# Forgetting attention with a feed-forward layer: q and k loads issued by GpSimd, the short chunk in rows 64 to 127, and x, inverse sums and output rows in one DMA each

## The chip, the cores and the metric

The kernel runs on one core of a Trainium2 chip. The metric is the device time of one execution in microseconds (us); of several runs the median counts. Engine names are those of the profile: PE is TensorE's matmul side and PEld its weight loads, DVE is VectorE, ACT is ScalarE, POOL is GpSimd, SP is SyncE, which issues nearly all DMAs of the kernel before.

## The reference

Eight batches with eight heads each, 576 positions, head size 64. The attention has a decay: for each head the cumulated log of a gate f is added to the scores. Its output, as 4608 tokens of 512 numbers, goes through a feed-forward layer of width 2048.

```python
scores = scale * np.matmul(q, k.transpose(0, 1, 3, 2))
log_f = np.log(np.clip(f, 0.0001, 1.0))
cum = np.cumsum(log_f, axis=-1)
decay = cum[:, :, :, None] - cum[:, :, None, :]
scores = np.where(causal, -1000000000.0, scores + decay)
attn = np.exp(scores - np.max(scores, axis=-1, keepdims=True))
attn = attn / (np.sum(attn, axis=-1, keepdims=True) + 1e-09)
x = np.matmul(attn, v)          # then to (B*S, H*D)
h = x @ w_in
out = np.maximum(0.01 * h, h) @ w_out
```

## The kernel before

**Precision.** Products are made in float32r with each operand split into a high part (a cast) and a low part (the rest): three matmuls per product. Casts are on ACT or DVE, the subtractions that give the low parts mostly on POOL (`minus`).

**Stages.** Until about 125 us weights are loaded and split, and the first 256 tokens of three batches are done in a way of their own. Then come 64 tasks, one per head: 40 full ones (576 queries in five chunks of 64, 128, 128, 128, 128 rows), until about 745 us, and 24 short ones (three chunks of 64, 128, 128 rows, the later queries of the three batches), until about 1095 us. The rest is feed-forward alone. Between the steps of the tasks, `fill` lays pieces of the feed-forward (h, g, gh, gl, o) on the engines, by a credit that is fixed when the program is built.

**A task.** Its scores (`sc`) come chunk by chunk from TensorE, DVE adds the mask and finds the maximum (`z`, `max`), ACT takes the exponential, DVE transposes 32x32 blocks into `zt`. SP sends `zt` to DRAM (`send`: four DMAs `zd<-zt`) and fetches it back transposed over partitions (`receive`: one DMA `fixed_pl<-zd`). ACT casts it to `fixed_ph`, DVE makes the low part in `fixed_pl` (`divide`), TensorE multiplies with the values (`av`), ACT copies one part out (`y`), DVE adds (`x`). A full task does this in two pieces (0 and 1), a short one in one. After each odd task the inverse sums of its pair of heads go through DRAM (`rt`, `inv`, `rb`), `x` is multiplied by them (`normalise`) and written to `xd`, from where the feed-forward reads it.

**The next tasks' data.** In the second half of each task q and k for the task after the next are loaded into `qraw` and `kraw` (one buffer each; `load`, four DMAs of 64 rows), after ACT has cast the next task's `s` and `m` from the same buffers (`split`) and ACT and POOL have made its `fixed_s2`/`fixed_m2` (`prepare`: ACT casts, POOL subtracts).

**Order.** Each engine runs its instructions in the order in which the code is written. `todo` places each step of a task in a slot (eight slots to a task): send of piece 0 in slot 3, receive 0 and send 1 in 5, `split_next`, `load_next` and `split_v` in 6, receive 1 in 9, values in 12 and 16, `prepare_next` in 2; in short tasks send in 5 and receive in 9. A DMA that must wait stops all that SP has behind it. A DMA also takes one of eight completion semaphores in turn (DMAHW0 to 7 for SP), and waits for the DMA that had it last where nothing else has made sure of that.

**Rows and columns.** x, the inverse sums and xd hold the tokens of a task permuted (32 rows of each chunk side by side), so an output tile of 128 rows consists of up to four runs of 32 tokens (`tokens`, `segments`) and is written with as many DMAs.

Since all engines are called through `Lane` (line 54), the profile gives that line for nearly all instructions; they are told apart by their tiles.

Of the kernel before, what the change touches and what calls it, by code (L numbers as in the profile page):

```python
# [70 lines left out]
def forgetting_attention_ffn(ctx, tc, qT, kT, v4, vr, f, w_in, w_out, out):  # L71
# [47 lines left out]
    def tokens(lo, hi):  # L119

        if hi - lo == T:
            return [(0, T)]
        runs = []
        for a in range(P // Q):
            for c in range(0 if lo == 0 else 2, NCH):
                at, m = max(ST[c], lo), width(c) - max(ST[c], lo)
                if a * Q < m:
                    runs.append((at + a * Q, Q))
        return runs
# [793 lines left out]
```

## Time and profile before

| | |
|---|---|
| time, three runs | 1213.93 us median (1209.92 to 1215.66) |
| profiled execution | 1214.48 us, its span 1212.5 us |
| mean granted TensorE clock | 0.976 |
| busy in the span: PE, DVE, ACT, POOL | 1138.8, 727.8, 707.5, 433.9 us |
| DMA | 156515 packets, 220.10 MB |
| 0 to 125 us, early part | PE busy 119.10 us |
| 125 to 745 us, full tasks | PE busy 573.34 us of 620.00 |
| 745 to 1095 us, short tasks | PE busy 334.30 us of 350.00 |
| 1095 to 1212.5 us, feed-forward alone | PE busy 112.02 us of 117.50 |

The span is the time from the first to the last instruction that the profiler saw; the time of the execution itself is 2 us more. Busy times of different engines lie beside each other, so they don't add up to the span.

### The profile page before, as it was taken

How to read it: one execution, taken by the hardware profiler on the slowest of the kernel's cores; microseconds unless marked ns; L12 is line 12 of the kernel's file. 1: busy time of each engine (PE TensorE's matmuls, PEld its weight loads, DVE VectorE, ACT ScalarE, POOL GpSimd, SP SyncE). 2: the span in 40 equal slices, each digit the busy share in tenths (PEclk: the TensorE clock that was granted, in tenths of full speed). 3: DMA queues.
4: the chain of work that ended last, by engine and by line, in shares of the span. 5: the costliest groups of instructions: out<-in, count | busy, mean ns of one | idle time of the engine just before them, and what ended most of it. 6: DMA issues, size and time to landing. Idle time of an engine off the chain costs nothing.

```text
span 1212.5 us, 22013 instructions
## 1 busy us (share of the span) xinstructions
PE 1138.8 (94%) x7148; PEld 1012.0 (83%) x7148; DVE 727.8 (60%) x1982; ACT 707.5 (58%) x1555; POOL 433.9 (36%) x350
## 2 busy tenths in 40 slices
PE   9999887879998999899998999999999998889998
PEld 6677776769897998889987999899989997778997
DVE  6888367766676666567666755655656665652221
ACT  7877467766666656666566665555556555641111
POOL 1000434434453544344443444343535443432000
PEclk9999889989998999999998999999999998999999
DMA  6654477877767776776767666656565657661000
GB/s 212 199 184 161 121 228 219 239 218 215 225 199 229 223 219 198 211 222 196 225 192 218 170 211 190 194 162 188 163 188 171 205 175 219 189 183 36 28 18 18
DMA packets 156515, 220.10 MB, mean 182 GB/s; under 512 B 27760, under 2 KB 117920, under 8 KB 156400
## 3 DMA queue, kind: packets, MB, share of 16 engines
q1 hardware_dynamic: 156400, 218.70, 60.8%
q8 instruction: 56, 0.92, 0.3%
q14 instruction: 59, 0.48, 0.1%
HBM read 141.87 MB, written 76.75 MB: 180 GB/s over the span
## 4 chain that ended last, share of the span: by engine, by line
PE 66%; DMA 12%; DVE 8%; ACT 7%; issue 4%; SPq 3%; POOL 1%; DVEq 0%; ACTq 0%; POOLq 0%
PE o L54 25%; PE h L54 24%; PE av L54 6%; DMA fixed_pl<-zd 5%; PE sc L54 5%; SPq L54 3%; DVE fixed_pl L54 3%; DMA kraw<-in_kT 2%; ACT fixed_ph L54 2%; DVE z L54 1%; PE ave L54 1%; PE sce L54 1%; PE warm L54 1%; ACT z L54 1%; DMA xd<-x 1%
## 5 line engine op out<-in xcount | busy, mean ns | idle before, releaser
L54 PE MATMUL h<-xh,win_h 128*128 128x256 f32 x1152 | 330.1, 287 | 0.4 <-ACT xh L54 0.4
L54 PE MATMUL h<-xh,win_l 128*128 128x256 f32 x1152 | 325.3, 282 | 0.0
L54 ACT ACTIVATE z<-z,max 64x64 f32<-64x64 f32 (+3 forms) x272 | 160.8, 591 | 229.9 <-DVE max L54 228.2
L54 PE MATMUL h<-xs,win_h 128*128 128x256 f32 x1024 | 288.6, 282 | 0.0
L54 PE MATMUL o<-wout_h,gh 128*128 128x512 f32 x576 | 234.2, 407 | 0.0
L54 PE MATMUL o<-wout_l,gh 128*128 128x512 f32 x576 | 230.1, 399 | 0.0
L54 PE MATMUL o<-wout_h,gl 128*128 128x512 f32 x576 | 229.1, 398 | 0.0
L54 PEld LDWEIGHTS h<-xh,win_h 128*128 128x128 f32 x1152 | 219.9, 191 | 5.7 <-ACT xh L54 0.9
L54 POOL TENSOR_TENSOR gl<-g,gh 128x512 fp32r<-128x512 f32 x119 | 155.3, 1305 | 187.7 <-DVE gh L54 142.0
L54 DVE TENSOR_TENSOR fixed_pl<-fixed_pl,fixed_ph 128x768 fp32r<-128x768 f32 x168 | 152.9, 941 | 113.6 <-ACT fixed_ph L54 113.6
L54 PEld LDWEIGHTS h<-xh,win_l 128*128 128x128 f32 x1152 | 219.6, 191 | 0.1
L54 DVE CUSTOM_DVE_ANT_0 z<-sc,tri 64x64 f32<-64x64 f32 (+3 forms) x272 | 122.6, 451 | 153.6 <-PE sc L54 149.4
L54 PEld LDWEIGHTS h<-xs,win_h 128*128 128x128 f32 x1024 | 195.2, 191 | 3.2
L54 DVE STREAM_TRANSPOSE zt<-z 64x64 f32<-64x64 f32 (+4 forms) x528 | 162.5, 344 | 25.4 <-ACT z L54 20.7
L54 ACT ACTIVATE g<-h 128x512 f32<-128x512 f32 x144 | 85.6, 594 | 144.9 <-PE h L54 135.3
L54 PE MATMUL sc<-m,s 128*128 128x64 f32 (+2 forms) x336 | 104.7, 317 | 46.9 <-ACT m L54 23.8
L54 ACT CAST fixed_ph<-fixed_pl 128x768 fp32r<-128x768 f32 x168 | 120.4, 754 | 44.5 <-DMA fixed_pl<-zd 44.1
L54 DVE CAST gh<-g 128x512 fp32r<-128x512 f32 x144 | 73.4, 510 | 119.7 <-ACT g L54 117.3
L54 PEld LDWEIGHTS o<-wout_h,gl 128*128 128x128 f32 x576 | 109.4, 190 | 26.1 <-POOL gl L54 0.2
L54 PEld LDWEIGHTS o<-wout_h,gh 128*128 128x128 f32 x576 | 109.6, 190 | 18.6 <-issue 0.5
L54 PEld LDWEIGHTS o<-wout_l,gh 128*128 128x128 f32 x576 | 109.8, 191 | 17.6 <-issue 0.3
L54 PEld LDWEIGHTS sc<-m,s 128*128 128x128 f32 x336 | 65.2, 194 | 64.7 <-ACT m L54 32.7
(115 smaller groups left out, 1665.3 us busy)
## 6 DMA issues: line engine op xcount, KB each, us to landing
zd<-zt SPq DMA_DIRECT2D x160, 144.0 KB
fixed_pl<-zd SPq DMA_DIRECT2D x40, 576.0 KB
kraw<-in_kT SPq DMA_DIRECT2D x128, 144.0 KB
zd<-zt SPq DMA_DIRECT2D x96, 192.0 KB
fixed_pl<-zd SPq DMA_DIRECT2D x24, 768.0 KB
zd<-zt SPq DMA_DIRECT2D x160, 96.0 KB
fixed_pl<-zd SPq DMA_DIRECT2D x40, 384.0 KB
qraw<-in_qT SPq DMA_DIRECT2D x80, 144.0 KB
```

What stands on the lines that cost most here:

```text
L54: ins = f(*args, **kw)
```

## The change

1. The chunk of 64 rows lies in rows (partitions) 64 to 127 of its tiles, no longer in 0 to 63. The tiles of q's parts are now fixed and 64 columns wider, with 64 columns of zeros in front, so that a chunk always takes 128 columns that end with its last query. A few memsets on POOL ahead of the tasks make these zeros.
2. x and the inverse sums lie in token order. So x goes to `xd` in one DMA and not two, an odd task's inverse sums in one and not two, and each output tile of 128 tokens in one DMA of 256 KB in place of (mostly) four of 64 KB. The multiplication by the inverse sums runs over 576 columns instead of 640 in full tasks.
3. The 256 loads of q and k of the tasks are issued by GpSimd (`nc.gpsimd`) and no longer by SP.
4. In `split` the cast of k (`m`) comes ahead of that of q (`s`).

The slots get names in tables (`PLANS`), all with the numbers of before; no step changes its slot.

```diff
     def load(t):
         for name, src, lo in (("q", qT, a), ("k", kT, 0)):
             x = h[name] = one.tile([P, S], F32, tag=f"{name}raw", name=f"{name}raw_{t}")
             for o in range(2):
-                nc.sync.dma_start(x[o * D:(o + 1) * D, lo:n], src[s][:, lo:n])
+                nc.gpsimd.dma_start(x[o * D:(o + 1) * D, lo:n], src[s][:, lo:n])
...
     def fix():
         for x in "ab":
             for w, n in (("s2", 2), ("m2", 4)):
-                y = fixed[w + x] = one.tile([P, S], F32R, tag=w + x, name=f"fixed_{w}{x}")
+                m = S + REST if w == "s2" else S
+                y = fixed[w + x] = one.tile([P, m], F32R, tag=w + x, name=f"fixed_{w}{x}")
                 nc.gpsimd.memset(y[:D].bitcast(F32), 0.0)
                 nc.gpsimd.memset(y[:n].bitcast(F32), 1.0)
+                if w == "s2":
+                    nc.gpsimd.memset(y[:, :REST].bitcast(F32), 0.0)
...
+        s1 = fixed["s1"] = one.tile([P, S + REST], F32R, tag="s1", name="fixed_s1")
+        nc.gpsimd.memset(s1[:, :REST].bitcast(F32), 0.0)
...
-    def split(t):
+    def split(t, which=0):
...
-        s1 = h["s1"] = one.tile([P, S], F32R, tag="s1", name=f"s1_{t}", bufs=1)
-        m1 = h["m1"] = one.tile([P, S], F32R, tag="m1", name=f"m1_{t}", bufs=1)
-        nc.scalar.copy(s1[:, a:n], h["q"][:, a:n])
-        nc.scalar.copy(m1[:, :n], h["k"][:, :n])
+        if "s1" not in h:
+            h["s1"] = fixed["s1"][:, REST:]
+            h["m1"] = one.tile([P, S], F32R, tag="m1", name=f"m1_{t}", bufs=1)
+        s1, m1 = h["s1"], h["m1"]
+        if which in (0, 2):
+            nc.scalar.copy(m1[:, :n], h["k"][:, :n])
+        if which in (0, 1):
+            nc.scalar.copy(s1[:, a:n], h["q"][:, a:n])
...
     def scores(t, i):
-        m, n, at = rows(t, i), width(i), begin(t, i)
+        m, n, at = rows(t, i), width(i), width(i) - P
+        part = slice(P - m, P)
         z = h[f"z{i}"] = one.tile([P, n], F32, tag="z" + "ab"[i % 2], name=f"z{i}_{t}")
-        z = z[:m]
+        z = z[part]
...
-                    ps[:, :b - a], h["s" + w][:, cols], h["m" + w][:, a:b],
-                    start=y == 0, stop=y == 1,
+                    ps[:, :b - a], fixed["s" + w + x2][:, n - P + REST:n + REST], h["m" + w][:, a:b],
+                    start=w == "1", stop=w == "2",
...
     def values(t, part):
-        x = pair["x"][:, :m * P].rearrange("p (a c) -> p a c", a=4)
+        x = pair["x"][:, :m * P].rearrange("p (c a q) -> p a c q", a=4, q=Q)
...
     def spread_inverse(t):
-        m = NCH - c0
-        for o in range(2):
-            to = inv[s // 2, o, :m * P].rearrange("(a c q) -> c a q", a=4, q=Q)
-            nc.sync.dma_start(to, rt[o * NCH + c0:(o + 1) * NCH].rearrange("c (a q) -> c a q", a=4))
+        nc.sync.dma_start(inv[s // 2].rearrange("o (c q) -> (o c) q", q=P), rt)
...
     def normalise(t):
-        nc.vector.tensor_tensor(x[:, :m * P], x[:, :m * P], r[:, :m * P], op=ALU.mult)
-        nc.sync.dma_start(to[:, :2 * m * Q], x[:, :2 * m * Q])
-        y = x[:, 2 * m * Q:4 * m * Q].rearrange("p (a c) -> p a c", a=2)[:, :, Q:]
-        nc.sync.dma_start(to[:, 2 * m * Q:].rearrange("p (a c) -> p a c", a=2), y)
+        n = slice(P - REST, m * P)
+        nc.vector.tensor_tensor(x[:, n], x[:, n], r[:, n], op=ALU.mult)
+        nc.sync.dma_start(to, x[:, n])
```

**Where instructions stand now.** POOL, in one of the first full tasks, before: the subtraction for the low part of v (`fixed_vs`), those for q and k of the next task (`qraw`, `fixed_m2a`), and one of the feed-forward (`gl`). The semaphores behind "waits" are those of the engines and of SP's DMAs (DMAHW).

```order
L54 TENSOR_TENSOR gl_6_1618<-g_6_1608,gh_6_1617 128x512 [waits DVE_49,Pool_49]
L54 TENSOR_TENSOR fixed_vs<-fixed_vm,fixed_vs 128x5x64 [waits DMAHW1_49,DMAHW0_49,Activation_49]
L54 TENSOR_TENSOR qraw_1631<-qraw_1631,fixed_s2a 64x576 [waits DMAHW4_49,DMAHW6_49,Activation_49,Pool_49]
L54 TENSOR_TENSOR fixed_m2a<-kraw_1634,fixed_m2a 64x576 [waits DMAHW0_49,PE_49,Activation_49]
L54 TENSOR_TENSOR gl_7_1704<-g_7_1689,gh_7_1703 128x512 [waits DVE_49,PE_49,Pool_49]
```

The same place on POOL in the changed kernel:

```order
L60 TENSOR_TENSOR gl_6_1621<-g_6_1611,gh_6_1620 128x512 [waits DVE_49,Pool_49]
L60 DMA qraw_1633<-in_qT 64x576 [waits DMASW4_49,Activation_49]
L60 DMA qraw_1633<-in_qT 64x576
L60 DMA kraw_1636<-in_kT 64x576 [waits DMASW6_49]
L60 DMA kraw_1636<-in_kT 64x576
L60 TENSOR_TENSOR fixed_vs<-fixed_vm,fixed_vs 128x5x64 [waits DMAHW1_49,DMAHW0_49,Activation_49]
L60 TENSOR_TENSOR qraw_1633<-qraw_1633,fixed_s2a 64x576 [waits DMASW1_49,Activation_49,Pool_49]
L60 TENSOR_TENSOR fixed_m2a<-kraw_1636,fixed_m2a 64x576 [waits DMASW3_49,PE_49,Activation_49]
L60 TENSOR_TENSOR gl_7_1706<-g_7_1691,gh_7_1705 128x512 [waits DVE_49,PE_49,Pool_49]
```

Four DMAs have come in ahead of `fixed_vs`, and the first of them waits for ACT's cast of `s`.

SP where a full task follows an odd one, before: the second `receive` of the odd task, two inverse-sum DMAs of its pair, the first `send` of the next task, the fetch of the inverse sums, the first `receive`.

```order
L54 DMA fixed_pl<-zd_128 128x1152 [waits DMAHW6_49,DMAHW7_49,DVE_49,PE_49]
L54 DMA fixed_s2b<-dec_q 2x576
L54 DMA fixed_m2b<-dec_k 2x576 [waits DMAHW0_49]
L54 DMA inv<-rt_2214 5x4x32 [waits DMAHW1_49,Activation_49]
L54 DMA inv<-rt_2214 5x4x32 [waits DMAHW2_49]
L54 DMA zd_127<-zt 32x4x192 [waits DMAHW3_49,DVE_49]
L54 DMA zd_127<-zt 32x4x192 [waits DMAHW4_49]
L54 DMA zd_127<-zt 32x4x192 [waits DMAHW5_49]
L54 DMA zd_127<-zt 32x4x192 [waits DMAHW6_49]
L54 DMA rb_2265<-inv 64x640 [waits DMAHW7_49,DMAHW1_49]
L54 DMA rb_2265<-inv 64x640 [waits DMAHW2_49,DMAHW0_49]
L54 DMA fixed_pl<-zd_127 128x768 [waits DMAHW5_49,DMAHW4_49,DMAHW6_49,DMAHW3_49,PE_49]
```

The same place on SP in the changed kernel:

```order
L60 DMA fixed_pl<-zd_128 128x1152 [waits DMAHW1_49,DMAHW6_49,DMAHW0_49,DMAHW7_49,DVE_49,PE_49]
L60 DMA fixed_s2b<-dec_q 2x576 [waits DMAHW5_49]
L60 DMA fixed_m2b<-dec_k 2x576
L60 DMA inv<-rt_2211 10x128 [waits Activation_49]
L60 DMA zd_127<-zt 32x4x192 [waits DVE_49]
L60 DMA zd_127<-zt 32x4x192
L60 DMA zd_127<-zt 32x4x192 [waits DMAHW2_49]
L60 DMA zd_127<-zt 32x4x192 [waits DMAHW3_49]
L60 DMA rb_2261<-inv 64x640 [waits DMAHW7_49,DMAHW4_49]
L60 DMA rb_2261<-inv 64x640 [waits DMAHW5_49]
L60 DMA fixed_pl<-zd_127 128x768 [waits DMAHW2_49,DMAHW3_49,DMAHW1_49,DMAHW6_49,DMAHW0_49,PE_49]
```

The load that stands first in both pieces is the eighth DMA ahead of the fourth `zd` before, and of the first `rb` now.

SP in two short tasks, before, from one `send` to the next task's:

```order
L54 DMA zd_128<-zt 32x4x384 x4
L54 DMA qraw_12105<-in_qT 64x320 x2
L54 DMA kraw_12108<-in_kT 64x576 x2
L54 DMA fixed_vm<-in_v 128x2x256
L54 DMA fixed_vm<-in_vr 64x2x64
L54 DMA xs_12132<-xd 128x4x256
L54 DMA fixed_pl<-zd_128 128x1536
L54 DMA fixed_s2b<-dec_q 2x320
L54 DMA fixed_m2b<-dec_k 2x576
L54 DMA inv<-rt_12174 3x4x32 x2
L54 DMA rb_12212<-inv 64x384 x2
L54 DMA zd_127<-zt 32x4x384 x4
```

The same place on SP in the changed kernel:

```order
L60 DMA zd_128<-zt 32x4x384 x4
L60 DMA fixed_vm<-in_v 128x2x256
L60 DMA fixed_vm<-in_vr 64x2x64
L60 DMA xs_11957<-xd 128x4x256
L60 DMA fixed_pl<-zd_128 128x1536
L60 DMA fixed_s2b<-dec_q 2x320
L60 DMA fixed_m2b<-dec_k 2x576
L60 DMA inv<-rt_11999 10x128
L60 DMA rb_12036<-inv 64x384 x2
L60 DMA zd_127<-zt 32x4x384 x4
```

The four loads of q and k no longer stand between `zd` and `fixed_pl`. The orders of PE, DVE and ACT are those of before but for the two casts that changed places and the shapes told above.

## Rows read from the trace of the kernel before

**Rows 1.** The page's head: the span, the busy time of each engine (with its share of the span and its number of instructions), and the shares of the engines in the chain of work that ended last.

```profile
span 1212.5 us, 22013 instructions
...
PE 1138.8 (94%) x7148; PEld 1012.0 (83%) x7148; DVE 727.8 (60%) x1982; ACT 707.5 (58%) x1555; POOL 433.9 (36%) x350
...
PE 66%; DMA 12%; DVE 8%; ACT 7%; issue 4%; SPq 3%; POOL 1%; DVEq 0%; ACTq 0%; POOLq 0%
```

**Rows 2.** Busy time by stretch, the full stage and the short one: the stretch and its length, then each engine's busy time with its instructions, the granted clock, the share of the DMA engines, GB/s.

```profile
125.00:745.00 620.00, 573.34 (x3667) 521.09 (x3666) 403.31 (x1174) 402.06 (x902) 266.34 (x204) 0.96 0.71 209
745.00:1095.00 350.00, 334.30 (x2092) 302.59 (x2091) 203.85 (x527) 195.80 (x411) 148.27 (x122) 0.99 0.62 185
```

**Rows 3.** The same view over the eleven stretches behind 125 us that ran at a granted clock near half: one of them, and the sum of all.

```profile
511.50:514.90 3.40, 3.40 (x18) 3.40 (x17) 2.88 (x11) 2.92 (x7) 1.49 (x2) 0.50 0.80 259
...
sum 57.80, PE 51.83 PEld 47.85 DVE 29.00 ACT 29.70 POOL 18.96; mean PE 4.71 PEld 4.35 DVE 2.64 ACT 2.70 POOL 1.72
```

**Rows 4.** What PE waited for, in the full stage (two rows) and in the short one (the last): us in total, times, longest.

```profile
PE sc L54 <- ACT m L54: 23.8, 13, 4.2
PE sc L54 <- DVE max L54: 17.0, 16, 3.3
...
PE av L54 <- ACT fixed_ph L54: 12.6, 10, 3.5
```

**Rows 5.** The same list for ACT, the full stage and then the short one.

```profile
ACT fixed_ph L54 <- DMA fixed_pl<-zd: 27.7, 20, 3.6
...
ACT fixed_ph L54 <- DMA fixed_pl<-zd: 16.4, 13, 3.3
```

**Rows 6.** Timeline of SP in a short task from `send` to `receive`: start, duration, the DMAs issued.

```profile
1020.14 2.12 SPq L54 DMA_DIRECT2D zd<-zt  x4
1022.30 1.47 SPq L54 DMA_DIRECT2D qraw<-in_qT  x2
1023.88 1.19 SPq L54 DMA_DIRECT2D kraw<-in_kT  x2
1025.30 0.40 SPq L54 DMA_DIRECT2D fixed_pl<-zd  x1
```

**Rows 7.** Timeline of SP and then of ACT in a full stretch with two inverse-sum DMAs: the same columns, and in brackets the idle time ahead and what ended it.

```profile
196.19 0.60 SPq L54 DMA_DIRECT2D inv<-rt  x2
197.07 3.23 SPq L54 DMA_DIRECT2D zd<-zt  x4
200.78 1.12 SPq L54 DMA_DIRECT2D rb<-inv  x2
202.07 0.45 SPq L54 DMA_DIRECT2D fixed_pl<-zd  x1
202.57 1.96 SPq L54 DMA_DIRECT2D zd<-zt  x4
...
206.05 0.83 ACT L54 CAST fixed_ph<-fixed_pl 128x768 fp32r<-128x768 f32 x1 [2.19 <-DMA fixed_pl<-zd]
```

**Rows 8.** Timelines of SP, ACT and PE in a full stretch with output rows.

```profile
500.78 1.78 SPq L54 DMA_DIRECT2D out<-ost  x4
...
503.86 0.52 SPq L54 DMA_DIRECT2D fixed_pl<-zd  x1
...
508.40 1.19 SPq L54 DMA_DIRECT2D kraw<-in_kT  x2
...
501.86 0.67 ACT L54 CAST s<-qraw 128x576 fp32r<-128x576 f32 x1
...
508.59 0.83 ACT L54 CAST fixed_ph<-fixed_pl 128x768 fp32r<-128x768 f32 x1 [3.59 <-DMA fixed_pl<-zd]
...
510.75 0.47 PE L54 MATMUL sc<-m,s 128*128 128x448 f32 x1 [3.34 <-DVE max L54]
```

**Rows 9.** Timelines of SP and ACT where output rows stand behind q and k.

```profile
161.82 1.18 SPq L54 DMA_DIRECT2D kraw<-in_kT  x2
163.10 1.00 SPq L54 DMA_DIRECT2D out<-part  x2
...
167.35 0.26 ACT L54 COPY rt<-rt 10x128 f32<-10x128 f32 x1 [2.00 <-DMA out<-part]
```

**Rows 10.** SP's issues of q and of output rows, by tile: count, and the duration in ns (smallest, median, largest).

```profile
L54 SPq DMA_DIRECT2D qraw<-in_qT x128: 471/596/1584, 125.1 to 1059.0; - x128
...
L54 SPq DMA_DIRECT2D out<-ost x120: 314/421/1541, 302.7 to 1209.5; - x120
```

**Rows 11.** Groups by line and shape: one of POOL's subtractions (busy us, mean ns of one, idle time before and what ended it), and TensorE's loads of weights for the products with gl.

```profile
L54 POOL TENSOR_TENSOR fixed_m2b<-kraw,fixed_m2b 64x576 fp32r<-64x576 f32 x32 | 47.4, 1481 | 0.1
...
L54 PEld LDWEIGHTS o<-wout_h,gl 128*128 128x128 f32 x576 | 109.4, 190 | 26.1 <-POOL gl L54 0.2
```

**Rows 12.** Two of DVE's groups from the page, with the same columns.

```profile
L54 DVE TENSOR_TENSOR fixed_pl<-fixed_pl,fixed_ph 128x768 fp32r<-128x768 f32 x168 | 152.9, 941 | 113.6 <-ACT fixed_ph L54 113.6
...
L54 DVE CAST gh<-g 128x512 fp32r<-128x512 f32 x144 | 73.4, 510 | 119.7 <-ACT g L54 117.3
```

**Rows 13.** Timelines of ACT and PE at the first task: the casts of s and m, and the first score matmul.

```profile
132.06 0.67 ACT L54 CAST s<-qraw 128x576 fp32r<-128x576 f32 x1 [0.94 <-POOL qraw L54]
132.64 0.67 ACT L54 CAST m<-kraw 128x576 fp32r<-128x576 f32 x1
...
133.36 0.42 PE L54 MATMUL sc<-m,s 128*128 128x64 f32 x1 [4.18 <-ACT m L54]
```

More of the change, by code (lines that the diff above doesn't have):

```diff
@@ L117, in forgetting_attention_ffn @@
         total += hi - lo
[L119 to L129, printed above, removed]
     where = []
     for b, lo, hi in blocks:
-        for at, m in tokens(lo, hi):
-            where += range(b * S + at, b * S + at + m)
+        where += range(b * S + lo, b * S + hi)
     def segments(n):
@@ L230, in forgetting_attention_ffn @@
     fc = one.tile([2 * NHEAD, S], F32, tag="qraw", name="fc")
-    pick = one.tile([P, NHEAD], F32R, tag="vt", name="pick")
+    pick = one.tile([P, NHEAD], F32R, tag="y", name="pick")
     both = one.tile([P, P + T], F32R, tag="kraw", name="both")
@@ L277, in later_decays, with places @@
                 nc.sync.dma_start(to[:, w], r[w * NHEAD:(w + 1) * NHEAD].bitcast(F32))
+    def places(t):
+        return PLANS[0 if t < NEAR else 2 if tasks[t][1] else 1]
     state = {}
@@ L496, in scores @@
             nc.vector.tensor_tensor_reduce(
-                out=z[:, a:b], in0=ps[:m, :b - a], in1=tri[:m, u:u + b - a], scale=-SCALE,
-                scalar=3.0e38 if x == 0 else h["max"][:m, i:i + 1],
-                op0=ALU.add, op1=ALU.min, accum_out=h["max"][:m, i + x:i + x + 1],
-            )
+                out=z[:, a:b], in0=ps[part, :b - a], in1=tri[part, u:u + b - a], scale=-SCALE,
+                scalar=3.0e38 if x == 0 else h["max"][part, i:i + 1],
+                op0=ALU.add, op1=ALU.min, accum_out=h["max"][part, i + x:i + x + 1],
+            )
+        if i == NCH - 1 and t + 1 < len(tasks) and places(t)["SIN"]:
+            split(t + 1)
         last = i + len(parts) - 1
         nc.scalar.activation(
-            z, z, AF.Exp, bias=h["max"][:m, last:last + 1], scale=-1.0,
-            accum_out=fixed["sum" + "ab"[s // 2 % 2]][:m, s % 2, i:i + 1],
+            z, z, AF.Exp, bias=h["max"][part, last:last + 1], scale=-1.0,
+            accum_out=fixed["sum" + "ab"[s // 2 % 2]][part, s % 2, i:i + 1],
         )
@@ L526, in turn @@
         h = state[t]
-        m = rows(t, i)
-        z = h[f"z{i}"][:m]
+        part = slice(P - rows(t, i), P)
+        z = h[f"z{i}"][part]
         js, groups_ = list(range(i)), []
@@ L599, in values @@
         nc.scalar.copy(y[mine], ps[other])
-        at = (lo - c0) * Q
-        h["add", part] = x[mine, :, at:at + k], out_[mine], y[mine].rearrange("p (a c) -> p a c", a=4)
+        h["add", part] = x[mine, :, lo - c0:hi - c0], *(
+            a[mine].rearrange("p (a c q) -> p a c q", a=4, q=Q) for a in (ps, y)
+        )
     def add(t, part):
@@ L846, in forgetting_attention_ffn @@
         odd = tasks[t][0] % 2
-        plan = [(6, split_next), (1, load_decay_next)] if t + 1 < nt else []
-        if part:
-            plan += [(3, send, 0), (5, receive, 0), (5, send, 1), (8, divide, 0, 0, 1),
-                     (12, values, 0), (13, add, 0), (9, receive, 1)]
-            for x, at in enumerate((13,13)):
-                plan.append((at, divide, 1, x, 2))
-            plan += [(16, values, 1), (17, add, 1)]
-            end = 18
-        else:
-            plan += [(5, send, 0), (9, receive, 0)]
-            for x, at in enumerate((13,13)):
-                plan.append((at, divide, 0, x, 2))
-            plan += [(16, values, 0), (17, add, 0)]
-            end = 18
-        plan += [(0, load_v), (6, split_v)]
+        w = places(t)
+        plan = [
+            (w["LV"], load_v), (w["SV"], split_v), (w["SB"], send, part),
+            (w["RB"], receive, part), (w["DB"], divide, part, 0, 2), (w["D2"], divide, part, 1, 2),
+            (w["VB"], values, part), (w["AB"], add, part),
+        ]
+        if part:
+            plan += [
+                (w["SA"], send, 0), (w["RA"], receive, 0), (w["DA"], divide, 0, 0, 1),
+                (w["VA"], values, 0), (w["AA"], add, 0),
+            ]
         if t + 1 < nt:
-            plan.append((2, prepare_next))
+            plan += [(w["PR"], prepare_next), (w["DEC"], load_decay_next)]
+            if not w["SIN"]:
+                plan.append((6, split_next))
         if t + 2 < nt:
-            plan.append((6, load_next))
+            plan.append((w["LD"], load_next))
         if odd:
-            plan += [(6, inverse), (10, spread_inverse), (12, fetch_inverse), (end, finish)]
+            plan += [
+                (w["IV"], inverse), (w["SI"], spread_inverse), (w["FI"], fetch_inverse), (w["NO"], finish),
+            ]
         for at, f, *args in plan:
```

19 lines of the change are left out of this document (12 added, 7 removed).

## The prediction

> **What bounds the kernel now.** I read the page first. TensorE is busy for 94% of the span and has 66% of the chain that ended last; DMA follows with 12% [rows 1]. So time comes from TensorE's gaps and from its clock, and everything else matters only through them. The table by stretch puts the gaps in the two attention stages: 620.00 − 573.34 = 46.7 us in the full one, 350.00 − 334.30 = 15.7 us in the short one [rows 2]. The list of TensorE's waits then names what ends them: in the full stage a score matmul that waits for ACT's cast of k (23.8 us, 13 times) or for DVE's score pass (17.0 us, 16 times), in the short stage a value matmul that waits for ACT's fixed_ph, 12.6 us in ten stalls [rows 4]. ACT's own list shows what is behind it: fixed_ph waits for the return trip of the probabilities through DRAM (zt → zd → fixed_pl), 27.7 us in 20 waits and 16.4 us in 13 [rows 5]. The clock comes last: eleven stretches, 57.8 us together, ran at a granted clock of 0.50, and half of the 51.83 us of matmul in them, 26 us, is what that cost [rows 3]. The stretch at 511.5 us begins 0.75 us after a gap of 3.34 us [rows 3, 8].
>
> So the question is when SP issues the load of fixed_pl, and what lies ahead of it in SP's order.
>
> **Short stage.** SP issues zd x4, q x2, k x2 and only then fixed_pl: zd ends at 1022.26, q and k take until 1025.07, fixed_pl starts at 1025.30, 3.0 us behind zd [rows 6]. How early could it start? In the full stage, where no q and k stand between, it started 202.07 − 200.30 = 1.8 us behind its zd, and this is a bound, since rb stood between [rows 7]. So q and k cost 1.2 us here, and on even tasks, where two loads of v remain ahead, about their own 2.5 us. Ten stalls have a mean of 1.26 us and a longest of 3.5 [rows 4]; nearly all are shorter than what is gained. I take 8 of the 12.6 us (bounds 0 and 12.6).
>
> **Full stage.** Here q and k stand behind the second zd group; the following fixed_pl has to wait for that group's landing anyway, and I count nothing for it. Three other things stand ahead of the first fixed_pl. (1) SP's completion lanes: with eight in rotation a DMA waits for the one issued eight before it. After the two inv the fourth zd waits for the landing of the fixed_pl load; four zd took 3.23 us against 1.96 for a free group [rows 7]. With one inv and no q and k it is rb, behind all zd, that waits for this load, so 1.3 us go from the path of the 19 full tasks that follow an odd one. (2) Four output DMAs of 32 rows took 1.78 us right ahead of fixed_pl [rows 8]; one DMA of the same bytes takes a median of 421 ns by the row of its issues [rows 10], so 1.3 us go where output rows lie in this place. (3) Output DMAs behind q and k held up ACT's rt once for 2.00 us [rows 9]; that wait goes. ACT waits 2.19 and 3.59 us for fixed_pl in the two places shown [rows 7, 8], so an earlier start is worth something, but only a part reaches TensorE: I let half of the 27.7 us go from ACT and a third of that, 5 us, from TensorE, plus the 2.0 of rt (bounds 0 and 27.7 + 2). The swapped casts spare the first task one cast: m could start at s's 132.06 instead of 132.64, 0.6 us of its 4.18 us gap [rows 13]. Together 7.6 us.
>
> **Clock.** With gaps of over 3 us shortened, one or two of the eleven stretches may go. I count one of 6.8 us, 3.4 us (bounds 0 and 26).
>
> **What POOL pays.** Four DMAs per task go in ahead of fixed_vs, gl, and the two subtractions: 256 in the 970 us of both stages. POOL is busy for 266.34 + 148.27 = 415 us of them [rows 2]. No DMA is issued by POOL before, so its price c is bounded: from below by SP's issue of the same transfers, 0.6 us median [rows 10], from above by POOL's own pass over a 64x576 tile, 1.48 us [rows 11]. Nothing in the trace lies between these ends; I take 1.0, the middle.
>
> The Trainium skill gives a first byte of about 1 us for a DMA that GpSimd issues and about 0.6 for one of SP ("DMA: Bandwidth & Descriptors", Latency and other measured facts); no row of before shows the first, and the second is what SP's row shows.
>
> At 1.0 POOL is busy for 415 + 256 = 671 of 970 us, 69%. What is late then? In the full stage SP ended k at 509.59, 7.1 us behind the cast of s [rows 8]; POOL would end 4.0 us behind it: earlier. In the short stage SP ends k 2.8 us behind the start of q [rows 6]; POOL would be 1.2 us later. gl comes behind the DMAs by up to 4 us, but a gl has a whole round of h and o matmuls as slack: TensorE waited 0.2 us for it in all [rows 11]. I laid the four DMAs into POOL's timeline of before, all else in place: lateness of gl beyond its need and of k's landing is 4.5 + 11 us in all at c = 1.0, 12 + 22 at 1.2, 32 + 51 at 1.5. These are estimates. Half of it, I assume, reaches TensorE: 8 us at 1.0, 17 at 1.2, 41 at 1.5. Two more for q and k that now move beside zd and fixed_pl, at a DMA share of 0.71 in the full stage [rows 2].
>
> The short chunk's place in rows 64 to 127, the additions in token order and the single x and inv DMAs change nothing else on TensorE: same matmuls, same shapes. The memsets are added in a stretch where POOL is idle.
>
> **Sum.** 8 + 7.6 + 3.4 = 19 gained, 8 + 2 = 10 paid: 9 us faster. The profiled execution took 1214.48 us (span 1212.5), 0.55 above the median of 1213.93. So 1205.5, and against the median 1205.
>
> **Rivals.**
> - *POOL becomes the late one (slower).* Gains of 19 are used up when half the lateness passes 17, at c of 1.2. At the upper bound of 1.48 it is 40: 1214.5 − 19 + 40 + 2 = 1237. For it: four DMAs in a row on an in-order queue ahead of the subtraction that the next task's scores need. Against it: POOL idles for over half of both stages. 0.20.
> - *POOL's DMAs stand still while VectorE works (slower).* If POOL could not write while DVE runs its passes over fixed_pl and gh, 152.9 + 73.4 = 226 us, 23% of 970 [rows 12], 1.0 becomes 1.3: lateness about 50, half of it 25, so 1214.5 − 19 + 25 + 2 = 1222. The Trainium skill has such a rule ("SBUF — State Buffer", SBUF: two separate sides): VectorE in its two-port mode locks GpSimd out of the shared port, so that its DMA descriptors are not written, 620 ns alone against some 3100 overlapped. Estimated from that page, if one DMA in five met such a pass, 256 x 0.2 x 2.5 = 128 us would be added on POOL, c of 1.5 and 1238. No row of before bears on it: POOL issues no DMA there. 0.05.
> - *The transfers are bound by landing, not by issue (no change).* fixed_pl started at 503.86 and ACT could use it only at 508.59, 4.7 us later [rows 8]; with that much in the transfer itself an earlier issue only moves the wait. TensorE then keeps most of its 12.6 and the clock its stretches: half of 16, 8, against 10 paid, with some chance for POOL at nothing: 1206 to 1216, say 1212. The Trainium skill leans this way: all issuing engines share the same 16 DMA engines, so spreading DMAs only saves issue time ("DMA: Bandwidth & Descriptors", Issuing engines are not separate DMA queues). 0.20.
> - *Both waits go.* All 12.6, half of the 27.7 on TensorE, 2.6 at rt and the start, half of the clock's 26, and POOL at the lower bound (2 paid): 1214.5 − 42 + 2 + 2 = 1176 at the end, 1186 for most of it. 0.10.
>
> **How the numbers follow.** My forecast holds 0.45, with 1196 to 1213 as its own range (c from 0.6 to 1.15). Half a percent, 6.1 us, is about what a measurement of this kernel tells from no change. Faster by more than that: 0.37 of the forecast, 0.10 of the large gain, 0.04 of no change: 0.51. Within it: 0.08 of the forecast, 0.13 of no change, 0.03 of POOL's at about 1.2: 0.24. Slower: 0.25. The range of 1186 to 1232 leaves out a tenth below, and the upper end of POOL's cost above.
>
> **What would show it.** Right: in the short stage fixed_pl starts within 2 us of zd's end (odd tasks), TensorE's wait for fixed_ph falls from 12.6 to about 5; four zd behind inv take 2 us, not 3.2; ACT's wait for fixed_pl in the full stage is about half; POOL's DMAs stand about 1 us apart; waits for gl and k stay under 10 us. Wrong: gaps of TensorE that end with gl, or ACT waiting for kraw in most tasks (POOL's price), ACT's wait for fixed_pl as before though issued earlier (landing), or a different number of half-clock stretches that outweighs all of it.

## The result and the profile after

The changed kernel takes 1222.19 us (median of 8 runs, 1220.14 to 1230.82) against 1213.99 for the kernel before (8 runs, 1209.92 to 1216.2): a ratio of 1.0075 with a 95% interval of 1.0047 to 1.0103. It is slower by 0.75%; the prediction had said 1205 us, 9 us faster. The profiled execution took 1221.93 us with a span of 1220.2, where that of before took 1214.48.

The page of the changed kernel: the span, the busy times, the chain that ended last, and the new DMA queue (packets, MB, share of 16 engines).

```profile
span 1220.2 us, 21805 instructions
...
PE 1144.4 (94%) x7148; PEld 1016.7 (83%) x7148; DVE 762.2 (62%) x1982; ACT 708.4 (58%) x1555; POOL 570.5 (47%) x609
...
q0 software_dynamic: 11520, 34.62, 9.4%
...
PE 62%; DMA 10%; DVE 9%; ACT 9%; issue 6%; POOL 3%; SPq 1%; DVEq 0%; ACTq 0%; POOLq 0%
```

Against [rows 1], POOL has 570.5 − 433.9 = 137 us more, which is its 256 DMAs. But DVE is also busy for 762.2 − 727.8 = 34 us more, with the same 1982 instructions, although the change makes one of its passes narrower. That was in none of the prediction's terms, and it is the first thing to follow.

By stretch, with the columns of [rows 2]:

```profile
125.00:745.00 620.00, 572.88 (x3633) 519.86 (x3632) 430.71 (x1160) 400.27 (x894) 349.91 (x364) 0.95 0.69 207
745.00:1095.00 350.00, 330.99 (x2063) 299.70 (x2064) 208.59 (x537) 194.91 (x412) 197.26 (x216) 0.98 0.60 183
```

TensorE's gaps are 47.1 and 19.0 us, against 46.7 and 15.7 in [rows 2]: the gaps that the change was to shorten have not become shorter in either stage. Most of DVE's extra time lies in the full stage, 430.71 against 403.31.

**Which passes of DVE grew.** Groups by line and shape (busy us, mean ns of one, idle time before), after, with POOL's DMAs; then the same DVE group of the kernel before.

```profile
L60 DVE TENSOR_TENSOR fixed_pl<-fixed_pl,fixed_ph 128x768 fp32r<-128x768 f32 x88 | 109.7, 1268 | 82.9 <-ACT fixed_ph L60 82.9
...
L60 POOL DMA_DIRECT2D qraw<-in_qT x128 | 68.7, 538 | 126.0 <-ACT fixed_vs L60 124.6 <-issue 0.4
L60 POOL DMA_DIRECT2D kraw<-in_kT x128 | 68.1, 534 | 10.5 <-PE sce L60 6.6 <-issue 0.4
```

```profile
L54 DVE TENSOR_TENSOR fixed_pl<-fixed_pl,fixed_ph 128x768 fp32r<-128x768 f32 x88 | 85.8, 997 | 95.7 <-ACT fixed_ph L54 95.7
```

One DMA costs POOL 0.53 to 0.54 us, less than the prediction's lower bound of 0.6; four are 2.1 us of a task. The 88 wide subtractions that make the low part of the probabilities took 1268 ns in place of 997, 23.9 us more in all: this one group is most of DVE's 34. Of the 88, 40 are the first pieces of the full tasks, one pass each; the other 48 belong to the short tasks, two passes each.

**What stands beside them.** The same place in both kernels, a full task near 162 us. First the kernel before, timelines of DVE and POOL (start, duration, instruction, in brackets the idle time ahead):

```profile
160.95 0.21 DVE L54 CUSTOM_DVE_ANT_0 z<-sc,tri 64x64 f32<-64x64 f32 x1
162.49 0.96 DVE L54 TENSOR_TENSOR fixed_pl<-fixed_pl,fixed_ph 128x768 fp32r<-128x768 f32 x1 [1.33 <-ACT fixed_ph L54]
163.37 0.35 DVE L54 CUSTOM_DVE_ANT_0 z<-sc,tri 128x192 f32<-128x192 f32 x1
...
159.68 0.89 POOL L54 TENSOR_TENSOR fixed_vs<-fixed_vm,fixed_vs 128x320 fp32r<-128x320 f32 x1 [2.21 <-ACT fixed_vs L54]
160.53 1.28 POOL L54 TENSOR_TENSOR gl<-g,gh 128x512 fp32r<-128x512 f32 x1
```

The same after, with SP's next load of v in the last row:

```profile
162.03 0.23 DVE L60 CUSTOM_DVE_ANT_0 z<-sc,tri 64x64 f32<-64x64 f32 x1
163.69 2.15 DVE L60 TENSOR_TENSOR fixed_pl<-fixed_pl,fixed_ph 128x768 fp32r<-128x768 f32 x1 [1.42 <-ACT fixed_ph L60]
165.87 0.36 DVE L60 CUSTOM_DVE_ANT_0 z<-sc,tri 128x192 f32<-128x192 f32 x1
...
160.69 1.08 POOL L60 DMA_DIRECT2D qraw<-in_qT  x2 [2.25 <-ACT fixed_vs L60]
161.80 1.07 POOL L60 DMA_DIRECT2D kraw<-in_kT  x2
162.88 0.90 POOL L60 TENSOR_TENSOR fixed_vs<-fixed_vm,fixed_vs 128x320 fp32r<-128x320 f32 x1
163.72 1.29 POOL L60 TENSOR_TENSOR gl<-g,gh 128x512 fp32r<-128x512 f32 x1
...
163.81 0.55 SPq L60 DMA_DIRECT2D fixed_vm<-in_v  x1
```

Before, POOL finished both subtractions at 161.81, 0.7 us ahead of DVE's. After, four DMAs push them behind 162.88, and DVE's pass now starts inside them. It ends at 163.69 + 2.15 = 165.84, which is 0.83 us behind the end of gl at 165.01. Another task shows the same, DVE and then POOL:

```profile
340.15 2.75 DVE L60 TENSOR_TENSOR fixed_pl<-fixed_pl,fixed_ph 128x768 fp32r<-128x768 f32 x1 [1.42 <-ACT fixed_ph L60]
...
339.95 0.89 POOL L60 TENSOR_TENSOR fixed_vs<-fixed_vm,fixed_vs 128x320 fp32r<-128x320 f32 x1
340.79 1.28 POOL L60 TENSOR_TENSOR gl<-g,gh 128x512 fp32r<-128x512 f32 x1
```

It ends at 342.90, and gl at 342.07: 0.83 us again. Of the 40 single passes of this shape in the full tasks thirteen took over 2 us, and all thirteen end 0.82 or 0.83 us behind the end of a gl. So DVE does not merely run slower beside POOL's subtractions: it stands until they are over. The Trainium skill says so ("SBUF — State Buffer", Who interferes with whom): a VectorE instruction with two SBUF inputs contends with a GpSimd instruction that reads SBUF, and the later one blocks fully. These rows agree for fixed_vs, which began first. But gl began up to 0.64 us after DVE's pass in twelve of the thirteen and still went ahead of it, which the page doesn't say. It is not always so: in two other passes, at 325.62 and 525.56, DVE went in between, and there gl took 2.00 and 2.01 us in place of 1.3.

What it costs in time: over the 40 full tasks, from the score pass of chunk 0 to that of chunk 1 (160.95 to 163.37 and 162.03 to 165.87 in the rows above) I sum 131.3 us before and 149.1 after, 17.8 more. The next two intervals win back 5.1 and 5.7, the others 1.6. The full tasks end 5.3 us longer (618.9 to 624.2), the short ones 4.7 (325.7 to 330.4).

**Who waits now.** TensorE, ACT and SP over the whole span (us, times, longest):

```profile
PE sc L60 <- DVE max L60: 23.8, 25, 2.3
PE sc L60 <- ACT fixed_s L60: 21.6, 10, 6.7
PE av L60 <- ACT fixed_ph L60: 11.0, 9, 3.5
...
PE o L60 <- POOL gl L60: 0.9, 1, 0.9
...
ACT fixed_ph L60 <- DMA fixed_pl<-zd: 25.6, 19, 3.4
...
ACT fixed_m2a L60 <- DMA kraw<-in_kT: 12.3, 11, 2.7
ACT fixed_s2a L60 <- DMA qraw<-in_qT: 9.1, 8, 3.4
...
SPq L60 <- DMA zd<-zt: 154.3, 131, 4.6
...
SPq L60 <- POOL fixed_vs L60: 89.5, 31, 5.7
```

ACT's wait for fixed_pl fell from 27.7 + 16.4 us [rows 5] to 25.6. In its place ACT's casts of q and k wait for their loads, 25.6 us in all four casts against 6.6 before. POOL's DMAs land 3.5 to 3.9 us after their issue (medians). And SP has a new wait: the load of v may overwrite fixed_vm only when POOL has read it for fixed_vs, and POOL now does that 2.1 us later. Behind the load of v stands fixed_pl.

SP and POOL in a short task with a load of v, after:

```profile
1013.95 1.95 SPq L60 DMA_DIRECT2D zd<-zt  x4
1019.00 0.58 SPq L60 DMA_DIRECT2D fixed_vm<-in_v  x1
...
1021.88 0.34 SPq L60 DMA_DIRECT2D fixed_pl<-zd  x1
...
1016.96 1.07 POOL L60 DMA_DIRECT2D kraw<-in_kT  x2
1018.09 0.88 POOL L60 TENSOR_TENSOR fixed_vs<-fixed_vm,fixed_vs 128x320 fp32r<-128x320 f32 x1
```

SP is free at 1015.90 and stands until 1019.00, the end of POOL's fixed_vs at 1018.97; fixed_pl starts 6.0 us behind zd. And in the short tasks without a load of v, SP spends the time freed of q and k on waiting for zd to land. SP's wait for zd in the short stage, before and then after:

```profile
SPq L54 <- DMA zd<-zt: 5.1, 4, 2.5
```

```profile
SPq L60 <- DMA zd<-zt: 38.2, 31, 4.3
```

From the end of zd to the start of fixed_pl the eleven of these tasks in which q and k used to stand there took a median of 2.88 us before and 2.97 after.

### The profile page after: what moved, and what is told of

The parts are those of the page before. It is cut to its first block, busy times and chain, and to the rows that moved or that the text cites. A ratio compares the mean times of both kernels' runs of the same rounds, so it can differ in the third digit from the quotient of the medians.

```text
span 1220.2 us, 21805 instructions
## 1 busy us (share of the span) xinstructions
PE 1144.4 (94%) x7148; PEld 1016.7 (83%) x7148; DVE 762.2 (62%) x1982; ACT 708.4 (58%) x1555; POOL 570.5 (47%) x609
## 4 chain that ended last, share of the span: by engine, by line
PE 62%; DMA 10%; DVE 9%; ACT 9%; issue 6%; POOL 3%; SPq 1%; DVEq 0%; ACTq 0%; POOLq 0%
PE o L60 23%; PE h L60 22%; PE av L60 6%; PE sc L60 5%; DMA kraw<-in_kT 3%; DMA fixed_pl<-zd 3%; DVE fixed_pl L60 2%; DVE z L60 2%; ACT fixed_ph L60 2%; DMA zd<-zt 2%; ACT z L60 2%; DVE zt L60 1%; SPq L60 1%; PE sce L60 1%; PE ave L60 1%
## 5 line engine op out<-in xcount | busy, mean ns | idle before, releaser
L60 DVE TENSOR_TENSOR fixed_pl<-fixed_pl,fixed_ph 128x768 fp32r<-128x768 f32 x168 | 175.3, 1074 | 97.2 <-ACT fixed_ph L60 97.1
L60 PE MATMUL sc<-m,fixed_s 128*128 128x64 f32 (+2 forms) x336 | 105.2, 318 | 51.5 <-DVE max L60 23.8
L60 ACT CAST fixed_ph<-fixed_pl 128x768 fp32r<-128x768 f32 x168 | 120.6, 755 | 26.8 <-DMA fixed_pl<-zd 25.6
L60 POOL DMA_DIRECT2D qraw<-in_qT x128 | 68.7, 538 | 126.0 <-ACT fixed_vs L60 124.6
```

Source lines behind the costliest of these rows:

```text
L60: ins = f(*args, **kw)
```

## Experiments

Two theories for the loss. **A:** the loads on POOL cost it, and the rest of the change gains. **B:** the new layout costs it, and the loads are harmless or good. Ratios are to the kernel before on the same chip, with 95% intervals. "Interval 0–1" is the sum from above, 131.3 us before, 149.1 after.

**e1: the change with q and k issued by SP.**

```diff
-                nc.gpsimd.dma_start(x[o * D:(o + 1) * D, lo:n], src[s][:, lo:n])
+                nc.sync.dma_start(x[o * D:(o + 1) * D, lo:n], src[s][:, lo:n])
```

> The changed kernel with the 256 loads of q and k issued by SP again; layout, single DMAs and the order of the casts stay changed. Theory A (the loads on POOL cost the time, through what they displace on POOL and through later landing): this kernel is faster than before, 1200 to 1210 us, DVE's busy time falls back from 762 to about 728 us, ACT's waits for qraw and kraw from 25 to about 6 us. Theory B (the layout costs it: one output DMA of 256 KB, runs of 32 in the additions): it stays at 1218 to 1226 us with DVE near 760.

Measured: 1207.8 us, 0.9939 (0.9911 to 0.9968). The layout alone gains 0.6%, so the loads on POOL cost 1.0075 − 0.9939 = 1.4%, some 16 us. Interval 0–1 is 134.0. Groups and waits of e1:

```profile
L60 DVE TENSOR_TENSOR fixed_pl<-fixed_pl,fixed_ph 128x768 fp32r<-128x768 f32 x88 | 86.0, 999 | 92.4 <-ACT fixed_ph L60 92.2
...
ACT fixed_ph L60 <- DMA fixed_pl<-zd: 36.7, 24, 3.8
```

DVE's pass is back at 999 ns. DVE as a whole is busy for 740.1 us and not for the 728 expected, so 12 of the 34 us came with the layout. ACT waits longer for fixed_pl than with the loads on POOL (36.7 against 25.6), and yet the kernel is faster.

**e2: the kernel before with only the loads on POOL.**

```diff
-                nc.sync.dma_start(x[o * D:(o + 1) * D, lo:n], src[s][:, lo:n])
+                nc.gpsimd.dma_start(x[o * D:(o + 1) * D, lo:n], src[s][:, lo:n])
```

> The kernel before with nothing changed but the 256 loads of q and k issued by GpSimd. Theory A: slower than before, 1220 to 1235 us, and slower than the whole change, since the gains of the layout are missing; DVE's mean for fixed_pl 128x768 rises from 997 to about 1270 ns. Theory B: 1205 to 1214 us.

Measured: 1221.9 us, 1.0050 (1.0027 to 1.0073): the move loses in the old layout too, though less; that it would be slower than the whole change was a miss. The two signs show here as well:

```profile
L54 DVE TENSOR_TENSOR fixed_pl<-fixed_pl,fixed_ph 128x768 fp32r<-128x768 f32 x88 | 96.8, 1122 | 95.9 <-ACT fixed_ph L54 94.6 <-DMA out<-ost 1.3
...
SPq L54 <- POOL fixed_vs L54: 66.7, 27, 4.6
```

e1 and e2 settle for A. What follows asks by which way.

**e3: the change, with fixed_vs ahead of the four DMAs on POOL.**

```diff
-        split_next, receive, send, load_next, inverse, spread_inverse, ...
+        split_next, receive, send, split_v, load_next, inverse, spread_inverse, ...
```

> The changed kernel with split_v ranked ahead of load_next, so that on POOL the subtraction of fixed_vs stands ahead of the four DMAs and not behind them. If the delay of fixed_vs is what costs (SP's load of fixed_vm waits for it 89.5 us in 31 waits, and fixed_pl stands behind): 1205 to 1214 us, that wait under 30 us. If later landing of q and k costs: not faster than the changed kernel, 1220 to 1230 us, ACT's waits for qraw and kraw over 25 us.

Measured: 1233.43 us, 1.0147 (1.0108 to 1.0186), worse still. SP's wait for fixed_vs fell to 25.9 us, but the DMAs start about 1 us later, and ACT's casts of q and k waited 54.6 us, 44 times. This speaks for the lateness of q and k as a second cause, though POOL's passes still meet DVE's here (interval 0–1 is 142.7).

**e4: e1 with twelve small copies on POOL where the DMAs stood.** It takes POOL's time without a transfer.

```diff
+        for _ in range(12):
+            nc.gpsimd.tensor_copy(fixed["s2" + "ab"[t % 2]][:1, :REST], fixed["s1"][:1, -REST:].bitcast(F32))
```

> As the first of these kernels (loads on SP), but POOL carries twelve small copies of 1x64 in the place where the changed kernel has its four DMAs, waiting for the same cast; they take POOL some 2 us per task and move no data of the task. If the time of the DMAs on POOL is what costs (its passes then fall beside DVE's pass over fixed_pl, and fixed_vs is late): as slow as the changed kernel, 1218 to 1226 us, DVE's busy time over 750. If it is the transfers themselves (software-issued, landing later): as fast as loads on SP without the copies.

Measured: 1242.02 us, 1.0206 (1.0166 to 1.0245). A copy took 264 to 278 ns, so POOL lost 3.2 us per task, half as much again as by the DMAs, and TensorE's wait for gl rose to 7.8 us. POOL's time alone can cost more than the whole loss, but the dose was too large.

**e7: the same with eight copies.** 8 x 268 ns is 2.1 us, the price of the four DMAs.

> Loads on SP, and eight small copies on POOL in the place of the four DMAs, 8 x 0.27 = 2.2 us per task, as long as the DMAs take there (the twelve of before took 3.2 us). If POOL's time alone explains the loss: 1219 to 1225 us. If half of it is landing: 1212 to 1217 us. ACT's waits for qraw and kraw stay near 6 us either way.

Measured: 1216.61 us, 1.0008 (0.9984 to 1.0033). Against e1, 2.1 us of POOL's time costs 0.7% (by the two intervals 0.3 to 1.1), about half of the 1.4% (1.0 to 1.8), with q and k still issued by SP. Interval 0–1 is 145.8.

```profile
L60 DVE TENSOR_TENSOR fixed_pl<-fixed_pl,fixed_ph 128x768 fp32r<-128x768 f32 x88 | 105.9, 1226 | 91.8 <-ACT fixed_ph L60 91.8
...
SPq L60 <- POOL fixed_vs L60: 14.4, 23, 1.8
```

DVE's pass is as long as after (1226 against 1268 ns), and no DMA of POOL is there. Nine single passes took over 2 us, and all nine end 0.82 us behind the end of a gl. So it is POOL's shifted subtractions, not its DMAs, that hold DVE.

**e5 and e6: q and k as one DMA of 128 rows each**, from inputs that hold them twice, on SP (e5, edit to e1) and on POOL (e6, edit to the change).

```diff
-            for o in range(2):
-                nc.gpsimd.dma_start(x[o * D:(o + 1) * D, lo:n], src[s][:, lo:n])
+            nc.sync.dma_start(x[:, lo:n], src[s][:, lo:n])
...
+        "q2": np.concatenate([q.reshape(B * H, S, D).transpose(0, 2, 1)] * 2, axis=1),
```

> Loads on SP as in the first experiment, but q and k of a task come as one DMA of 128 rows each (from copies of q and k in DRAM that hold each head twice), so two issues per task and not four, with the same bytes. If SP's issue time ahead of fixed_pl is worth something (1.2 us less in each task): 1200 to 1206 us against 1207.8. If the transfers bound it: 1206 to 1210 us.

> The changed kernel, loads on POOL, with one DMA of 128 rows for each of q and k: POOL gives 1.1 us per task instead of 2.1, the same bytes move. If POOL's time (fixed_vs late, passes beside DVE) costs the 14 us that lie between the changed kernel and loads on SP: about half comes back, 1212 to 1217 us. If the late landing of these transfers costs them: 1219 to 1224 us, with ACT's waits for qraw and kraw still near 25 us.

Measured: e5 1199.49 us, 0.9885 (0.985 to 0.992), the fastest of all; e6 1211.84, 0.9970 (0.9947 to 0.9994). Half the DMAs are worth about 0.5% on SP and 1% on POOL, and POOL still loses 0.9% to SP. e5's waits:

```profile
PE av L60 <- ACT fixed_ph L60: 7.9, 7, 2.9
...
ACT fixed_ph L60 <- DMA fixed_pl<-zd: 22.0, 18, 3.2
```

With two issues less on SP, ACT's wait for fixed_pl is lower than with all four moved to POOL (25.6), and nothing is paid on POOL. In e6 a wide DMA takes 538 (k) to 556 ns (q) of POOL but lands later, the KB and the median us to landing being the last numbers here:

```profile
kraw<-in_k POOLq DMA_DIRECT2D x64, 288.0 KB, 4.5
qraw<-in_q POOLq DMA_DIRECT2D x40, 288.0 KB, 4.7
```

**e8: e1 with x and inverse sums in two DMAs and output rows in DMAs of 32 rows**, all else as changed.

```diff
-        nc.sync.dma_start(to, x[:, n])
+        nc.sync.dma_start(to[:, :w], x[:, P - REST:P - REST + w])
+        nc.sync.dma_start(to[:, w:], x[:, P - REST + w:m * P])
...
-                    nc.sync.dma_start(out[row:row + m, :], o[x:x + m])
+                    for y in range(0, m, Q if n > 2 else m):
```

> Loads on SP and the changed layout, but x and the inverse sums go in two DMAs again and each output tile in four of 32 rows, as many as before the change. If the smaller number of SP's issues is what made the layout faster: back to 1212 to 1217 us. If something else in it did (the order of the two casts, the short chunk's place): 1206 to 1210 us.

Measured: 1218.39 us, 1.0019 (0.9994 to 1.0044), the median of ten executions, one of which took 1550.83. The gain of e1 is gone: it is the smaller number of DMAs, not the chunk's place in rows 64 to 127. ACT waited 42.0 us for fixed_pl.

**e9: the change with the load of v behind fixed_pl in SP's order**, in all three plans:

```diff
-    dict(SA=3, SB=5, ..., SV=6, LV=0, IV=6, ...),
+    dict(SA=3, SB=5, ..., SV=6, LV=1, IV=6, ...),
```

> The changed kernel, with the loads of v one slot later, so that SP issues fixed_pl ahead of them: SP's wait for POOL's fixed_vs (89.5 us in 31 waits in the changed kernel) no longer stands ahead of fixed_pl. If this wait is how the DMAs on POOL reach TensorE: 1208 to 1215 us, ACT's wait for fixed_pl under 20 us. If the passes beside DVE and the late landing of q and k are the way: 1218 to 1224 us, with DVE's mean for fixed_pl 128x768 still above 1200 ns.

Measured: 1224.3 us, 1.0060 (1.0037 to 1.0083), the same as the change.

```profile
SPq L60 <- POOL fixed_vs L60: 4.1, 3, 2.0
```

SP's new wait is gone, and nothing measurable is gained. But interval 0–1 is 160.6 here, 11.5 us more than after, so another part grew and the edit does not isolate the wait.

**e10 and e11: e9's edit with 128-row loads, on POOL and on SP.**

> Loads on POOL as two DMAs of 128 rows per task, and v behind fixed_pl. In the two-DMA kernel on POOL ACT waited 40 us for fixed_pl and only 6 us for qraw and kraw, so here the wait of SP for fixed_vs is nearly all that is left: 1200 to 1206 us if it is what holds fixed_pl up, 1209 to 1213 us if not.

> Loads on SP as two DMAs of 128 rows per task, v behind fixed_pl: SP's 1.2 us for the loads of v leave the path of fixed_pl in every even task. 1193 to 1199 us if ACT's remaining 22 us of waiting for fixed_pl fall by half; 1198 to 1202 us if the landing of zd sets it.

Measured: e10 1221.4 us, 1.0044 (1.0024 to 1.0063), a miss: it is worse than e6. e11 1201.06, 0.9873 (0.9845 to 0.9901), the same as e5.

**e12 to e15: POOL's fixed_vs earlier**, so that it is over ahead of the DMAs: the change (e12), e1 (e13), e6 (e14), e5 (e15).

```diff
-    dict(SA=3, SB=5, ..., SV=6, LV=0, IV=6, ...),
+    dict(SA=3, SB=5, ..., SV=4, LV=0, IV=6, ...),
```

> The changed kernel with split_v two slots earlier (slot 4): POOL's pass over fixed_vs stands ahead of ACT's casts of k and q and so ahead of the four DMAs, which stay right behind these casts. In the changed kernel 29.6 us of POOL's passes fall beside DVE's subtractions of fixed_pl 128x768 between the first and second score pass of the full tasks (2.1 before), which take 59.8 us instead of 38.6, and the whole interval 149.1 instead of 131.3. If this collision is what costs: the sum goes back to about 40 us, the interval to about 130, the time to 1207 to 1213 us. If the DMAs themselves or the landing of q and k cost it: 1218 to 1224 us.

> The control: loads on SP, layout changed, split_v two slots earlier. No DMA pushes fixed_vs here, so by the collision theory nothing to gain: 1205 to 1211 us as with slot 6 (1207.8). If an early fixed_vs gains on its own, this falls as far as the kernel with the loads on POOL.

> Loads on POOL as two DMAs of 128 rows, split_v two slots earlier. By the collision theory 8.8 us of overlap are left to remove against 29.6: 1206 to 1210 us (1211.8 with slot 6).

> Loads on SP as two DMAs of 128 rows, split_v two slots earlier, so that SP's load of fixed_vm no longer waits for POOL's fixed_vs (9.9 us): 1196 to 1200 us by the collision theory (1199.5 with slot 6).

Measured: e12 1234.8 us, 1.0159 (1.0132 to 1.0186); e13 1211.96, 0.9995 (0.9975 to 1.0015); e14 1214.65, 0.9995 (0.9978 to 1.0011); e15 1205.96, 0.9933 (0.9907 to 0.996). e12, e13 and e15 are slower than without the edit; e14's 0.25% is within the noise. In e12 interval 0–1 is back at 136.2, but the other piece pays, the pass over 576 columns that took 860 ns after:

```profile
L60 DVE TENSOR_TENSOR fixed_pl<-fixed_pl,fixed_ph 128x576 fp32r<-128x576 f32 x80 | 78.2, 1016 | 28.7 <-ACT fixed_ph L60 28.7
```

The same shows in e13 (1007 ns), without any DMA on POOL: the edit moves the meeting to another pass. So it doesn't isolate the first one.

**e16 and e17: fixed_vs on DVE**, in the change (e16) and in e1 (e17).

```diff
-        minus(vs[:, :, D:], vm, vs[:, :, :D].bitcast(F32))
+        nc.vector.tensor_tensor(vs[:, :, D:], vm, vs[:, :, :D].bitcast(F32), op=ALU.subtract)
```

> The changed kernel with the subtraction of fixed_vs on DVE (right ahead of the first score pass) and no longer on POOL: no pass of POOL stands behind the four DMAs to fall beside DVE's subtraction of fixed_pl; DMAs and landing stay. If the collision costs most of the 14 us: DVE's sum over fixed_pl 128x768 between the first two score passes back from 59.8 to about 40 us and the time 1210 to 1216 us, within 6 us of its control. If landing costs most of them: 1218 to 1226 us, 10 us or more above its control.

> The control: loads on SP, changed layout, fixed_vs's subtraction on DVE. The pass itself costs DVE some 0.45 us in each task ahead of the first score pass: 1207 to 1213 us.

Measured: e16 1221.06 us, 1.0033 (1.0007 to 1.0060); e17 1205.65, 0.9914 (0.9874 to 0.9955). The gap between loads on POOL and on SP is still 1.2%, although interval 0–1 is 128.5 in e16 and SP no longer waits for POOL's fixed_vs. What is left in e16, and in the last row the same DVE group in e17:

```profile
L60 DVE TENSOR_TENSOR fixed_pl<-fixed_pl,fixed_ph 128x768 fp32r<-128x768 f32 x88 | 97.5, 1130 | 72.0 <-ACT fixed_ph L60 72.0
...
ACT fixed_m2b L60 <- DMA kraw<-in_kT: 11.8, 8, 3.8
ACT fixed_m2a L60 <- DMA kraw<-in_kT: 10.2, 8, 2.9
...
L60 DVE TENSOR_TENSOR fixed_pl<-fixed_pl,fixed_ph 128x768 fp32r<-128x768 f32 x88 | 86.7, 1007 | 79.1 <-ACT fixed_ph L60 79.1
```

The expectation left out gl: it too stands behind the four DMAs and still meets DVE. The 40 single passes take 49.5 us in e16 and 39.0 in e17, against 62.4 after and 38.7 in e1, so the meeting is halved and not gone, and interval 0–1 is 122.7 in e17. ACT's casts of q and k wait 33.9 us in all (7.7 in e17). The last interval of a full task, from the last score pass to the next task's first, grew from 246.1 after to 260.2 us; but in e17 it is 254.1 against 247.0 in e1, so half of that growth is the subtraction's new place on DVE. With the meeting halved the gap is 1.2%, within the noise still the 1.4% of e1 against the change. So the meeting, which e7 shows to cost time, is probably not the only cause; late q and k are a candidate for the rest, which no run here isolates.

**e18: e1 with the cast of q ahead of that of k.**

```diff
-        if which in (0, 2):
-            nc.scalar.copy(m1[:, :n], h["k"][:, :n])
         if which in (0, 1):
             nc.scalar.copy(s1[:, a:n], h["q"][:, a:n])
+        if which in (0, 2):
+            nc.scalar.copy(m1[:, :n], h["k"][:, :n])
```

> Loads on SP, changed layout, with the cast of q ahead of that of k as before the change. The swap was counted at 0.6 us: 1207 to 1210 us, not to be told from 1207.8.

Measured: 1206.72 us, 0.9925 (0.9896 to 0.9954), the same as e1.

## Why the prediction was wrong, step by step

**Short stage, 8 us: wrong.** The step that failed is the bound of 1.8 us for fixed_pl behind zd, read in the full stage [rows 7], where a zd of the first piece carries 96 KB; in the short stage it carries 192. In the short stage fixed_pl waits for zd to land, and q and k had only filled that time: 2.88 us with them, 2.97 without. In tasks with a load of v, which were to gain 2.5 us, the wait for fixed_vs took the place (median 4.67 us before, 5.15 after). TensorE's wait for fixed_ph went from 12.6 to 11.0 us, not to 5. The rival of landing was right on this term.

**Full stage, 7.6 us: near in size for the layout, lost in the sum.** In the place of [rows 7] four zd behind the inverse sums take 2.02 us (predicted 2, before 3.23). But that place was one of the longest: over all such groups the median was 2.08 us before and 1.78 after, so most of the 19 tasks had 0.3 us to gain there and not 1.3. The wait of rt for output rows is gone; ACT's wait for fixed_pl in the full stage fell to 14.3 us, about half of 27.7, as forecast. Yet only part of that came from the layout: with loads on SP (e1) it is still 26.0, and e1 gains 0.6%, some 7 us. e8 shows that this gain comes with the number of DMAs. The other part of the halved wait is the moved loads, and TensorE got nothing of it: in the same stage q's and k's casts now wait 15.9 us, and DVE's passes are 27 us longer. The swap of the casts (0.6 us) is too small to be seen (e18).

**Clock, 3.4 us: not in the changed kernel.** The profiled execution had a granted clock of 0.970 against 0.976. From 125 to 1095 us it had fourteen stretches at half clock, with 62.89 us of matmul, against eleven with 51.83 [rows 3]; by the prediction's own reckoning that is 5.5 us more and not 3.4 less. The eight runs had 0.968 to 0.976, with a median of 0.974. With the loads on SP a gain does show: the median of e1's seven runs is 0.979, that of the 18 runs of the kernel before beside them 0.973. Over 1208 us this difference is some 7 us (an estimate), as much as e1 gains; with e8's DMAs the median is 0.974 again. So the layout gained by the clock, or with it, and the loads on POOL took that back.

**What POOL pays, 8 + 2 us: the step that turned the sign.** The price c was too high (0.53, taken 1.0), and gl was late for TensorE by 0.9 us only, so the rival of a late POOL fell in the form it was given. By the text's own reckoning such a price should have cost about 2 us; the measured cost is some 16. The mistake was to lay the DMAs into POOL's timeline "all else in place" and to ask only who waits for POOL's results. I didn't ask which engine works beside the passes that are shifted. [Rows 11, 12] had both sides, POOL's passes with two inputs and DVE's 152.9 us of fixed_pl, as busy times only; where they stood to each other, 0.7 us apart, was in the timeline and not looked at. e7 shows that such a shift alone costs about half of the loss, and at a clock of 0.979 (median of ten runs) as in e1. q and k were late as well: 11 us of lateness were forecast for k at c of 1.0, and at half that price the casts of q and k waited 25.6 − 6.6 = 19 us more. Their lateness was taken from the time of issue alone; how long POOL's loads take to land (3.9 us) was not in it. The 0.6 us of SP's row [rows 10], set there beside a first byte, is how long SP takes to issue a DMA; no row shows when the first byte comes.

**POOL's DMAs stand still while VectorE works: no.** Medians of 532 and 518 ns, the longest 1.09 us. The block that cost time went the other way, DVE behind POOL.

**Both waits go: no.** TensorE's gaps stayed.

**What stays open.** Half of the 16 us is not settled. Late q and k, SP's wait for fixed_vs and the clock remain for it; each edit that reduced one of them (e3, e9, e12, e16) let another grow, so I can't say how it is shared out. The clock is the one with a size: 0.974 after against 0.979 in e1 and e7 is some 6 us (an estimate), but what lowered it is not shown. Late q and k are not needed for a loss: in e6 their casts wait 6.4 us only, and it still loses 0.9% to e5, at nearly the same clock (medians 0.9775 and 0.9785). There SP's wait for fixed_vs is 51.1 us against 9.9, and ACT's for fixed_pl 40.0 against 22.0; e10 took SP's wait away and was no faster.

## What to carry to other kernels

When work is put into an idle engine's queue, look at what it pushes back, and at which engine works beside the pushed passes: about half of this loss came from two subtractions on POOL that moved 2.1 us, into a VectorE pass with two SBUF inputs, though TensorE hardly waited for them. An issue taken off a queue is worth nothing where the next one has to wait for a landing anyway; read the wait behind it first. Fewer DMAs on the same queue (e1, and e5 with q and k laid twice in DRAM: 1199.49 us, 1.2% faster than before) beat the same DMAs on another one.
